# Attention, a routed and a dense feed-forward in one kernel: side work of the weights taken at full pace behind the routing, and one scale worked out inside it

## Chip, cores and metric

The kernel runs on one core of a Trainium2 chip. The metric is the device time of one execution in microseconds; of several runs the median counts. Time before: 695.2 us, median of three runs (694.49 to 697.42).

## What is computed

Three parts follow each other, for 3072 tokens of 384 values:

```python
# 1: linear attention, 4 batches, 8 heads, 768 steps, 48 values a head
cur   = einsum('bhd,bhe->bhde', u * kt, vt)
y[t]  = einsum('bhd,bhde->bhe', rt, state + cur)
state = w * state + einsum('bhd,bhe->bhde', kt, vt)
# 2: routing: all (token, expert) logits in falling order; a token goes to the first
#    of 8 experts that still has room (384 tokens each)
logits = x @ w_gate
h = maximum(x[mask] @ w1[e], 0); out[mask] = h @ w2[e]      # F = 1024
# 3: dense, with w1, w2, w3 of 384 x 768 and w_out of 768 x 384
h = maximum(maximum(x @ w1, x @ w2), x @ w3); out = h @ w_out
```

All of it is float32. The products of parts 2 and 3 run in float16 with each operand as a high and a low half, so one product is three matmuls for each 128 rows of the contraction: high by high, low by high, high by low. A matrix therefore needs **side work** before its first use: it is loaded in blocks of 768 KB, its largest magnitude is found, a power of two is made of that as its scale, and it is split into halves.

## The kernel before, in words

Attention comes first (to about 160 us), then the routing, which works on 24 x 8 logits a partition (to about 198 us), then the eight experts one after another, each with its share of part 3. TensorE (PE) does the products, ScalarE (ACT) the high halves, VectorE (DVE) the low halves, GpSimd (POOL) gathers and scatters of tokens, SyncE (SP) issues the loads.

**An expert** has four steps, in class Experts. `first` (8 products of nine matmuls, L925-932) gives the hidden layer, whose halves `ht` ACT and DVE write. `second` (3 products of 24, L934-962) gives `x`, whose scale DVE works out from the peaks `part` ("layer" scale). `third` (6 groups of 3 products of nine, L964-985) multiplies by the three matrices V. Of a group, ACT takes the first product out of its bank (`top`, L977), DVE the other two (L979); then ACT and POOL write the halves `gt`. Three banks `pg` hold these products, so each product waits until the one three before it is taken out. `fourth` (3 times 18 matmuls into `px`, L987-1013) multiplies by the output matrix WO. For the first expert `first` is written chunk by chunk of 128 tokens: five banks are filled from each chunk while `turn` (L863-897) writes the chunk's halves `xt`.

**Side work** is a list, made by the planner `Feed` (L497-578) when the program is written, and so is the order of every engine. `weight` (L643-704) gives the items of one expert's matrix: four squares on ACT that find the peak (`look`), three items of the scale (`scaled`: collect, share, done), then splits (`upper` on ACT, L684, `lower` on DVE, L688). `double` (L706-788) gives those of a V or of WO, which come as 64-bit numbers and are made float32 first: `magnitude` on ACT, `shift` (L739), `low` (L746) and `sign` (L755) on DVE, then squares, scale, splits (L780, L783). `Feed.take` (L562) runs items between the products against a budget of time: `side` (L1026) works out a pace from how much is left and when it is due (by tags: 0.2 the second expert's second matrix, 1 the last V, 1.5 WO, 2 and on the later experts), and what a step spends over its budget is carried as a debt to the next. `flush` runs all that is left of a tag. Four buffers `stage` hold the blocks; `Feed.ahead` (L538) writes a block's load into SP's queue when its first use is at most 6 items off and its buffer's last use is written.

In the routing, three `round`s and `settle` run on DVE and PE in turn. Between their steps stand `idle` steps of a generator, `inputs` (L812-828), which works out the scale of the tokens, and of the first four squares of the second expert's second matrix, two in each of the first two rounds (`aside`, L1262). A branch (L1411) skips more rounds, which the data does not need.

```python
        def side(time, part=1.0):
            clock[0] += time
            pace = max((feed.rest(tag) / max(due(tag) - clock[0] - SLACK[0] - SLACK[1] * feed.waits(tag), time) for tag in tags
                        if tag <= limit[0] and feed.left(tag)), default=0.0)
            feed.take(limit[0], min(SLACK[2] * pace * time, part * room[time]), None, time, APART)
```

Of the kernel before, what the change touches and what calls it, by code (L numbers as in the profile page):

```python
# [496 lines left out]
class Feed:  # L497


    SLOTS, AHEAD, LAG = 4, 6, 1.4  # L500

    def __init__(self):
        self.items, self.blocks, self.cost, self.at, self.loaded, self.spare, self.plan = [], [], [], 0, 0, 0.0, []
        self.now, self.ready = 0.0, 0.0

# [22 lines left out]
    def close(self):  # L528
        for tag, f, pe, blocks, cost in self.plan:
            self.cost.append((self.cost[-1] if self.cost else 0.0) + cost)  # L530
            for b in blocks:
                if b.first is None:
                    b.first = len(self.items)
                    self.blocks.append(b)
                b.last = len(self.items)
            self.items.append((tag, f, pe))
        self.plan = []

    def ahead(self, most=99):
        while self.loaded < min(most, len(self.blocks)):  # L540
# [45 lines left out]
class Experts:  # L586
# [53 lines left out]
    def mark(self, st):  # L640
        st["sent"] = self.feed.now

    def weight(self, e, which):  # L643

        nc = self.nc
        st = {"sent": 0.0}
        if which == 0:
            src, kb, n, store = self.w1d, self.KD, F, self.W1
            blocks = [self.block(src, e * DM * F + j * 512, [[F, 128], [128 * F, kb], [1, 512]], False)
                      for j in range(2)]  # L650
        else:
            src, kb, n, store = self.w2d, self.KF, DM, self.W2
            blocks = [self.block(src, e * DM * F + j * 4 * 128 * DM, [[DM, 128], [128 * DM, 4], [1, DM]], False)
                      for j in range(2)]

        def look(j):
            def go():
                if j == 0:
                    st["peaks"] = self.wp.tile([128, 4], F32, name=f"wpeak{which}")
                self.square(blocks[j // 2].get()[:, j % 2 * 768:j % 2 * 768 + 768], st["peaks"][:, j:j + 1])  # L660
                if j == 3 and not self.early:
                    self.mark(st)
            return go

        def column(out):
            nc.vector.tensor_reduce(out, st["peaks"], AX.X, OP.max)

        def powers(top):
            yield from self.sc.powering(top, 3, True, st)
            st["w"] = self.wpool[e % 2].tile([128, 2, kb, n], F16, name=f"w{which}", bufs=1)  # L670
            store[e] = (st["w"], st["f"])

        def part(j, q):
            if which == 0:
                return blocks[j].get()[:, q * 512:q * 512 + 512], [st["w"][:, t, q, j * 512:j * 512 + 512] for t in range(2)]
            k = 4 * j + 2 * q
            return blocks[j].get()[:, q * 768:q * 768 + 768], [
                st["w"][:, t, k:k + 2].rearrange("p k n -> p (k n)") for t in range(2)]

        parts = [(j, q) for j in range(2) for q in range(3 - which)]  # L680

        def upper(n):
            raw, (hi, _) = part(*parts[n])
            nc.scalar.activation(hi, raw, AF.Copy, scale=st["s"])  # L684

        def lower(n):
            raw, (hi, lo) = part(*parts[n])
            nc.vector.scalar_tensor_tensor(lo, raw, st["s"], hi, op0=OP.mult, op1=OP.subtract)  # L688

        def split(n):  # L690
            def go():
                if n < len(parts):
                    upper(n)
                if n:
                    lower(n - 1)
            return go

        def uses(n):
            return [blocks[parts[i][0]] for i in (n - 1, n) if 0 <= i < len(parts)]

        looks = [(look(j), False, [blocks[j // 2]], 0.9) for j in range(4)]
        return (looks + self.scaled(st, column, powers, blocks)
                + [(split(n), st if n == 0 and not self.early else False, uses(n), 0.6 + 0.3 * which)
                   for n in range(len(parts) + 1)])

# [105 lines left out]

    def inputs(self):  # L812

        sc, K = self.sc, self.K
        nc, peak, out = self.nc, sc.tile(), {}
        nc.vector.tensor_reduce(peak, K.norms, AX.X, OP.max)
        yield
        p = sc.psum()
        nc.tensor.transpose(p[:1, :128], peak, K.identf)
        yield  # L820
        most = sc.tile(shape=(1, 1))
        nc.vector.tensor_reduce(most, p[:1, :128], AX.X, OP.max)
        p = sc.psum()
        nc.tensor.matmul(p[:, :1], K.onesf[:1, :], most, start=True, stop=True)
        yield
        yield
        yield from sc.powering(p[:, :1], 7, True, out)
        K.xs, K.xf = out["s"], out["f"]

    def plan(self, late):  # L830

        feed = self.feed = Feed()
        self.early = False
        parts = [(0.2, self.weight(1, 1), None)] + [(1, self.double(i), 0) for i in late]
        parts[-1] = (1, parts[-1][1] + [(self.common, False, [], 1.5)], None)
        parts.append((1.5, self.double(3), 0))
        for e in range(2, E):
            parts += [(e, self.weight(e, 0), 7), (e + 0.3, self.weight(e, 1), 6)]
        feed.chain(parts)
        feed.close()  # L840
        feed.ahead(Feed.SLOTS)

    def open(self, ctx):
        tc = self.tc
# [65 lines left out]
            return self.psum.tile([128, CAP], F32, name="pg", bufs=3)  # L910
        return self.psum.tile([128, CAP], F32, name="ps", bufs=2)

    def first(self, e, wide=False, ahead=0):

        nc = self.nc
        h = self.act.tile([128, 2, self.KF, CAP], F16, name="ht", bufs=1)
# [1 line left out]
        w = self.W1[e][0]  # L918
        ps = [self.bank(f, wide) for f in range(ahead)]
        if ahead:  # L920
            for a, _ in enumerate(self.turn(e, True)):
                for f in range(ahead):
                    self.product(ps[f], w, slice(f * 128, f * 128 + 128), self.XT[e], self.KD,
                                 slice(a * 128, a * 128 + 128))
        for f in range(self.KF):  # L925
            if f < ahead:
                p = ps[f]
# [83 lines left out]
    def run(self):  # L1011
# [14 lines left out]
        def side(time, part=1.0):  # L1026

            clock[0] += time
            pace = max((feed.rest(tag) / max(due(tag) - clock[0] - SLACK[0] - SLACK[1] * feed.waits(tag), time) for tag in tags
                        if tag <= limit[0] and feed.left(tag)), default=0.0)  # L1030
            feed.take(limit[0], min(SLACK[2] * pace * time, part * room[time]), None, time, APART)

# [7 lines left out]
                feed.run()  # L1040

        self.gather(1)
        first = self.first(0, True, 5)
        for _ in range(5):
            next(first)
            clock[0] += F1
# [54 lines left out]
class Routing:  # L1101
# [11 lines left out]
    def fill(self):  # L1113
# [12 lines left out]
        part = t("part", [128, 1], I32)  # L1126
        nc.gpsimd.iota(part, [[0, 1]], base=0, channel_multiplier=1)
        self.i128 = count("i128", [[1, 128]], [128, 128], F16)
        self.token = t("token", [128, NT], F16)
        nc.gpsimd.iota(self.token, [[C, NT]], base=-N // 2, channel_multiplier=1, allow_small_or_imprecise_dtypes=True)  # L1130
        self.i24 = count("i24", [[1, NT]], [128, NT], F16)
        i8 = count("i8", [[0, J], [1, E]], [128, J, E])
        i25 = count("i25", [[1, NT + 1]], [128, NT + 1])
# [133 lines left out]
    def settle(self):  # L1267
# [32 lines left out]
        with nc.allow_low_precision(reason="whole numbers of up to 12 bits"):  # L1300
# [9 lines left out]
        nc.vector.tensor_tensor(col, af[:, :, None].to_broadcast([128, NT, NT]),  # L1310
                                self.i24[:, None, :].to_broadcast([128, NT, NT]), OP.is_equal)
        bent = col.rearrange("p (m q) n -> p m q n", q=4)[:, :, 2]
        nc.gpsimd.tensor_tensor(bent, bent, self.token.rearrange("p (m q) -> p m q", q=4)[:, :, 2, None]
                                .to_broadcast([128, NT // 4, NT]), OP.mult)
        rows = []
        for m in range(NT):
# [181 lines left out]
```

## Time and profile before

| | before |
|---|---|
| median of three runs | 695.2 us |
| the profiled execution, its time | 698.42 us |
| its span, first to last instruction | 696.7 us |
| PE busy | 650.7 us, 93% |
| DVE busy | 401.3 us, 58% |
| ACT busy | 351.8 us, 50% |
| POOL busy | 241.9 us, 35% |
| mean granted TensorE clock | 0.95 |

Times of rows are microseconds from the span's start. PE is the matmuls, PEld the weight loads beside them. A row of a timeline gives start, length, engine, line, operation, output<-input and how many instructions were merged; in brackets stands how long the engine sat idle before it, and what ended that. A row with a count is the whole stretch of these instructions. A granted clock of 1.00 is 2.4 GHz, of 0.50 it is 1.2 GHz.

### The profile page before, as it was taken

The numbers are of one execution on the slowest core, as the hardware profiler recorded it, in microseconds if no ns is written. First come the engines' busy times: TensorE is split into PE (matmuls) and PEld (weight loads), VectorE is DVE, ScalarE is ACT, GpSimd is POOL, SyncE is SP. The second block draws the span as 40 slices with busy tenths as digits, with TensorE's granted clock in tenths as the row PEclk, the third lists the DMA queues.
The fourth block names the chain that finished last, engine by engine and source line by source line (L and its number), as shares of the span: only waits on it lengthen the run. The fifth ranks groups of instructions, "written<-read, shape, count | busy, mean of one in ns | idle before, by whom it ended". The sixth has DMA issues, their size and how long they took to land.

```text
span 696.7 us, 14406 instructions
## 1 busy us (share of the span) xinstructions
PE 650.7 (93%) x5667; PEld 432.2 (62%) x5667; DVE 401.3 (58%) x1055; ACT 351.8 (50%) x785; POOL 241.9 (35%) x271
## 2 busy tenths in 40 slices
PE   6999998998689998799999999999999999999996
PEld 4788787887476554356666656666665666666663
DVE  7687997785715957646466454635636553551321
ACT  3576566643415556367466547446464535342321
POOL 6999999970150003113023112202212111110222
PEclk9889999996569999799999999999999999999999
DMA  8876867503035516116134310620611220000000
GB/s 225 277 254 215 291 207 229 177 35 115 1 107 123 184 45 176 39 69 159 49 123 87 117 58 24 162 88 35 156 48 70 46 92 1 34 1 1 35 1 34
DMA packets 54763, 72.98 MB, mean 105 GB/s; under 512 B 21408, under 2 KB 42016, under 8 KB 54688
## 3 DMA queue, kind: packets, MB, share of 16 engines
q1 hardware_dynamic: 51616, 62.55, 29.0%
q0 software_dynamic: 3072, 9.44, 4.8%
q8 instruction: 46, 0.75, 0.4%
q14 instruction: 29, 0.24, 0.1%
HBM read 58.41 MB, written 9.44 MB: 97 GB/s over the span
## 4 chain that ended last, share of the span: by engine, by line
PE 54%; issue 7%; DVE 5%; ACT 4%; POOL 1%; POOLq 0%; DVEq 0%; ACTq 0%
PE pg L904 25%; PE ps L904 20%; PE px L997 8%; ACT w L684 1%; DVE top L979 1%; POOL gt L984 1%; ACT junk L617 1%; DVE da L746 1%; DVE x2s L960 0%; ACT gt L983 0%; DVE ht L932 0%; DVE v L783 0%; DVE sc L430 0%; DVE da L739 0%; POOL out_dram L1002 0%
## 5 line engine op out<-in xcount | busy, mean ns | idle before, releaser
L904 PE MATMUL pg<-x2s,v 128*128 128x384 f16 x1296 | 218.2, 326 | 5.3 <-ACT top L977 3.3
L904 PEld LDWEIGHTS <-v 128*128 128x128 f16 x1296 | 126.6, 98 | 90.9 <-issue 6.0
L984 POOL TENSOR_TENSOR gt<-top,gt 128x384 f16<-128x384 f32 x48 | 44.5, 927 | 349.2 <-ACT gt L983 295.6
L904 PEld LDWEIGHTS <-w 128*128 128x128 f16 x1242 | 117.4, 99 | 73.7 <-issue 2.3
L688 DVE SCALAR_TENSOR_TENSOR w<-stage,sc,w 128x512 f16<-128x512 f32 (+1 forms) x80 | 72.4, 930 | 59.2 <-ACT w L684 59.2
L979 DVE SCALAR_TENSOR_TENSOR top<-pg,sc,top 128x384 f32<-128x384 f32 x96 | 59.1, 615 | 74.3 <-PE pg L904 63.6
L904 PE MATMUL ps<-ht,w 128*128 128x384 f16 x576 | 94.9, 326 | 1.7 <-DVE ht L932 1.7
L904 PE MATMUL ps<-xt,w 128*128 128x384 f16 (+1 forms) x540 | 88.8, 318 | 0.2 <-ACT xt L895 0.2
L997 PE MATMUL px<-wo,gt 128*128 128x384 f16 x432 | 76.4, 337 | 5.9 <-ACT wo L780 2.3
L983 ACT ACTIVATE gt<-top 128x384 f16<-128x384 f32 x48 | 25.1, 522 | 109.5 <-DVE top L979 109.5
L997 PEld LDWEIGHTS <-gt 128*128 128x128 f16 x432 | 43.1, 101 | 38.0 <-issue 9.2
L684 ACT ACTIVATE w<-stage,sc 128x512 f16<-128x512 f32 (+1 forms) x80 | 61.4, 798 | 2.2 <-DVE sc L468 2.2
L617 ACT ACTIVATE junk<-stage 128x768 bf16<-128x768 f32 x64 | 53.6, 838 | 5.1 <-DMA stage<-in_moe_w_dram 4.1
L932 DVE SCALAR_TENSOR_TENSOR ht<-ps,ht 128x384 f16<-128x384 f32 x56 | 31.0, 555 | 32.2 <-ACT ht L931 32.1
L1002 POOL DMA_INDIRECT out_dram<-o,ids x24 | 23.9, 995 | 47.1 <-ACT o L1000 47.1
L977 ACT ACTIVATE top<-pg,sc 128x384 f32<-128x384 f32 x48 | 27.7, 577 | 20.7 <-PE pg L904 18.2
L230 DVE TENSOR_TENSOR am<-pA,mask 128x512 f32<-128x512 f32 x48 | 30.7, 680 | 8.6 <-PE pA L227 8.6
L943 ACT ACTIVATE x<-ps 128x384 f32<-128x384 f32 x24 | 11.8, 491 | 47.0 <-PE ps L904 47.0
L931 ACT ACTIVATE ht<-ps 128x384 f16<-128x384 f32 x56 | 26.8, 482 | 15.8 <-PE ps L904 15.4
L1000 ACT ACTIVATE o<-px,sc 128x384 f32<-128x384 f32 x24 | 13.9, 581 | 39.1 <-PE px L997 35.8
L129 POOL TENSOR_TENSOR rt<-rt,tr 128x512 f32<-128x512 f32 x22 | 33.5, 1524 | 0.0
L227 PE MATMUL pA<-rt,kt 64*128 64x128 f32 x384 | 30.1, 292 | 2.2 <-DVE am L230 1.9
(236 smaller groups left out, 876.6 us busy)
## 6 DMA issues: line engine op xcount, KB each, us to landing
stage<-in_moe_w_dram SPq DMA_DIRECT2D x41, 768.0 KB, 5.3
kn<-in_k_dram SPq DMA_DIRECT2D x24, 192.0 KB, 5.1
rn<-in_r_dram SPq DMA_DIRECT2D x24, 192.0 KB, 4.9
v<-in_v_dram SPq DMA_DIRECT2D x24, 192.0 KB, 3.3
rt<-in_rt_dram SPq DMA_DIRECT2D x48, 96.0 KB, 3.4
x_rows<-x SPq DMA_DIRECT2D x24, 192.0 KB, 2.7
stage<-in_moe_w_out_dram SPq DMA_DIRECT2D x3, 768.0 KB, 5.6
xg<-x_rows,ids POOLq DMA_INDIRECT x24, 4.2
```

The lines of the kernel that those rows point to most:

```text
L129: (engine or self.nc.gpsimd).tensor_mul(self.RT[i], self.RT[i], self.tr)
L227: nc.tensor.matmul(pa[s][:, j, :], kt[FULL[s], j * C:(j + 1) * C], rt[FULL[s], j * C:(j + 1) * C], start=True, stop=True, skip_group_check ...
L230: nc.vector.tensor_mul(am[:, s], pa[s], self.mask[:, None, :].to_broadcast([128, NP, C]))
L617: self.nc.scalar.activation(self.K.junk, x, AF.Square, accum_out=total)
L684: nc.scalar.activation(hi, raw, AF.Copy, scale=st["s"])
L688: nc.vector.scalar_tensor_tensor(lo, raw, st["s"], hi, op0=OP.mult, op1=OP.subtract)
L904: nc.tensor.matmul(p[:, rows], w[:, wi, k, cols], x[:, xi, k, rows], start=k == 0 and wi + xi == 0, stop=k == kb - 1 and xi == 1, skip_gro ...
L932: nc.vector.scalar_tensor_tensor(h[:, 1, f], p, 0.0, h[:, 0, f], op0=OP.max, op1=OP.subtract)
L977: nc.scalar.activation(t, p, AF.Copy, scale=self.ratio[i])
L979: nc.vector.scalar_tensor_tensor(t, p, self.ratio[i], top, op0=OP.mult, op1=OP.max)
L984: nc.gpsimd.tensor_sub(gt[:, 1, g], top, gt[:, 0, g])
L997: nc.tensor.matmul(p, gt[:, gi, g, a * 128:(a + 1) * 128], self.WO[:, wi, g, :], start=g == 0 and gi + wi == 0, stop=g == self.KG - 1 and ...
```

## The change

Five things, all in what is written where:

1. In the routing the generator `inputs` goes on after the tokens' scale with the same steps for the second expert's second matrix (`self.later`, a call of the new `across`), so that its scale is worked out in the third round by two small products on PE. The items collect, share and done leave the list.
2. Eight items of side work are written into the first expert's `first` by a new argument `between`: one split before the chunks, four more behind the second chunk (these are all five of the second expert's second matrix), three of the last V behind the third.
3. `side` takes pace 1 as long as anything up to WO (tag 1.5) is left.
4. This list's loads may be written 12 items ahead (the attention's list keeps 6), and the first four are written at once (`fill`, where `ahead` wrote those that are needed within 6 items).
5. `settle` multiplies by `tokf` in float32 on POOL, where it used a float16 copy `token`, which is no longer made.

```diff
-    SLOTS, AHEAD, LAG = 4, 6, 1.4
-    def __init__(self):
+    SLOTS, LAG = 4, 1.4
+    def __init__(self, ahead=6):
+        self.AHEAD = ahead
...
+    def fill(self):
+        while self.loaded < min(self.SLOTS, len(self.blocks)):
+            self.blocks[self.loaded].load()
+            self.loaded += 1
...
-    def weight(self, e, which):
+    def weight(self, e, which, routed=False):
...
-        return (looks + self.scaled(st, column, powers, blocks)
+        if routed:
+            self.later = lambda: self.across(column, powers)
+        return (looks + ([] if routed else self.scaled(st, column, powers, blocks))
...
     def inputs(self):
+        K, out = self.K, {}
+        yield from self.across(lambda t: self.nc.vector.tensor_reduce(t, K.norms, AX.X, OP.max),
+                               lambda top: self.sc.powering(top, 7, True, out))
+        K.xs, K.xf = out["s"], out["f"]
+        yield
+        yield from self.later()
+
+    def across(self, column, powers):
         sc, K = self.sc, self.K
-        nc, peak, out = self.nc, sc.tile(), {}
-        nc.vector.tensor_reduce(peak, K.norms, AX.X, OP.max)
+        nc, peak = self.nc, sc.tile()
+        column(peak)
         yield
...
-        yield from sc.powering(p[:, :1], 7, True, out)
-        K.xs, K.xf = out["s"], out["f"]
+        yield from powers(p[:, :1])
...
-        feed = self.feed = Feed()
+        feed = self.feed = Feed(12)
...
-        parts = [(0.2, self.weight(1, 1), None)] + [(1, self.double(i), 0) for i in late]
+        parts = [(0.2, self.weight(1, 1, True), None)] + [(1, self.double(i), 0) for i in late]
...
-        feed.ahead(Feed.SLOTS)
+        feed.fill()
...
-    def first(self, e, wide=False, ahead=0):
+    def first(self, e, wide=False, ahead=0, between=lambda a: None):
...
         if ahead:
+            between(-1)
             for a, _ in enumerate(self.turn(e, True)):
...
+                between(a)
...
-            pace = max((feed.rest(tag) / max(due(tag) - clock[0] - SLACK[0] - SLACK[1] * feed.waits(tag), time) for tag in tags
+            pace = 1.0 if feed.left(1.5) else max((feed.rest(tag) / max(due(tag) - clock[0] - SLACK[0] - SLACK[1] * feed.waits(tag), time) for tag in tags
...
-        first = self.first(0, True, 5)
+        first = self.first(0, True, 5, lambda a: self.aside({-1: 1, 1: 4, 2: 3}.get(a, 0)))
...
-        self.token = t("token", [128, NT], F16)
-        nc.gpsimd.iota(self.token, [[C, NT]], base=-N // 2, channel_multiplier=1, allow_small_or_imprecise_dtypes=True)
...
-        nc.gpsimd.tensor_tensor(bent, bent, self.token.rearrange("p (m q) -> p m q", q=4)[:, :, 2, None]
+        nc.gpsimd.tensor_tensor(bent, bent, self.tokf.rearrange("p (m q) -> p m q", q=4)[:, :, 2, None]
```

Lines of the changed kernel are up to 17 higher for the same code. The order of three places follows.

DVE at the end of the third round (`pick` is the last step of the round's search, `pen` the first that uses its result `pt`, which PE makes of `pick`). Before:

```order
L1250 SCALAR_TENSOR_TENSOR hit,pick<-rank,goal 96x8
L1256 SCALAR_TENSOR_TENSOR val,pick<-hit,top 96x8
L1258 SCALAR_TENSOR_TENSOR pick<-pick,least 96x1
L1264 TENSOR_TENSOR pen<-nl,pt 128x192
L1265 SCALAR_TENSOR_TENSOR nl<-pen,nl 128x192
L1271 TENSOR_REDUCE best<-nl 128x24
```

Changed:

```order
L1265 SCALAR_TENSOR_TENSOR hit,pick<-rank,goal 96x8
L1271 SCALAR_TENSOR_TENSOR val,pick<-hit,top 96x8
L1273 SCALAR_TENSOR_TENSOR pick<-pick,least 96x1
L838 TENSOR_REDUCE sc_3034<-px 1x1
L454 TENSOR_SCALAR sc_3038<-px 128x1
L1279 TENSOR_TENSOR pen<-nl,pt 128x192
L1280 SCALAR_TENSOR_TENSOR nl<-pen,nl 128x192
L1286 TENSOR_REDUCE best<-nl 128x24
```

Two steps of the scale now stand between `pick` and `pen`: the largest of 128 peaks, and the first step of the power, which reads a `px` that PE writes in between from the former.

DVE from the second expert's tokens (`xr`) to its first hidden values (`ht`); `w` is the second expert's second matrix, `da` and `wo` the last V on its way to float32, and the rows from L949 (L966) on the first expert's layer scale. Before, from the matrix's splits on (ahead of them stand `xr` and the steps of the matrix's scale):

```order
L688 SCALAR_TENSOR_TENSOR w_4494<-stage,sc_4487,w_4494 128x768 x4
L739 TENSOR_SCALAR da<-da 128x768
L746 SCALAR_TENSOR_TENSOR da<-stage,da 128x768
L755 SCALAR_TENSOR_TENSOR wo<-stage,da 128x768
L422 MEMSET sc_4569 128x32
L949 TENSOR_REDUCE sc_4569<-part 128x1
L430 STREAM_TRANSPOSE sc_2826<-sc_4569 32x32 x4
L431 TENSOR_REDUCE sc_4570<-sc_2826 32x1
L932 SCALAR_TENSOR_TENSOR ht<-ps,ht 128x384
```

Changed:

```order
L892 SCALAR_TENSOR_TENSOR xr<-xg_2819,sc_2926,xr 128x384
L763 SCALAR_TENSOR_TENSOR wo<-stage,da 128x768
L747 TENSOR_SCALAR da<-da 128x768
L754 SCALAR_TENSOR_TENSOR da<-stage,da 128x768
L763 SCALAR_TENSOR_TENSOR wo<-stage,da 128x768
L422 MEMSET sc_4572 128x32
L966 TENSOR_REDUCE sc_4572<-part 128x1
L430 STREAM_TRANSPOSE sc_2824<-sc_4572 32x32 x4
L431 TENSOR_REDUCE sc_4573<-sc_2824 32x1
L949 SCALAR_TENSOR_TENSOR ht<-ps,ht 128x384
```

The four splits and their scale have left this place (they stand in the first expert's `first`), and the last V is two `sign` steps along.

ACT from the second expert's last hidden values to its third step; `junk,peaks<-wo` are squares of the last V, `x` and `junk,part` the three products of `second`, `v` the last V's high halves, `top` the first product of the first expert's `third`, `da` the magnitudes of WO. Before:

```order
L931 ACTIVATE ht<-ps 128x384
L943 ACTIVATE x_4706<-ps 128x384
L944 ACTIVATE junk,part<-ps 128x384
L617 ACTIVATE junk,peaks_4563<-wo 128x768 x2
L943 ACTIVATE x_4706<-ps 128x384
L944 ACTIVATE junk,part<-ps 128x384
L943 ACTIVATE x_4706<-ps 128x384
L944 ACTIVATE junk,part<-ps 128x384
L780 ACTIVATE v_84<-wo,sc_4778 128x768 x3
L977 ACTIVATE top_4838<-pg,sc_4823 128x384
L724 ACTIVATE da<-stage 128x768
```

Changed:

```order
L623 ACTIVATE junk,peaks_4415<-wo 128x768
L948 ACTIVATE ht<-ps 128x384
L960 ACTIVATE x_4718<-ps 128x384
L961 ACTIVATE junk,part<-ps 128x384
L960 ACTIVATE x_4718<-ps 128x384
L961 ACTIVATE junk,part<-ps 128x384
L788 ACTIVATE v_84<-wo,sc_4752 128x768 x3
L960 ACTIVATE x_4718<-ps 128x384
L961 ACTIVATE junk,part<-ps 128x384
L994 ACTIVATE top_4837<-pg,sc_4822 128x384
L732 ACTIVATE da<-stage 128x768 x2
```

The last two squares have moved ahead of the last `ht`, the three `v` ahead of the third product, and a second magnitude of WO stands right behind the first.

## Rows read from the trace of the kernel before

**Rows 1.** Busy time by stretch: start:end, length, busy us (instructions) of each engine, clock, DMA.
```profile
core 0: us, PE busy (x) PEld busy (x) DVE busy (x) ACT busy (x) POOL busy (x), PEclk, DMA share, GB/s
198.00:237.40 39.40, 38.81 (x315) 27.33 (x316) 22.94 (x60) 19.07 (x38) 5.34 (x6) 0.93 0.54 152
...
256.90:282.70 25.80, 22.95 (x135) 13.14 (x135) 20.59 (x46) 16.04 (x32) 8.23 (x8) 1.00 0.49 138
...
289.50:300.20 10.70, 10.70 (x49) 5.63 (x49) 4.02 (x21) 1.17 (x3) 2.16 (x4) 0.73 0.10 38
...
308.70:690.00 381.30, 379.60 (x2331) 227.64 (x2330) 183.81 (x498) 184.36 (x373) 72.56 (x95) 1.00 0.22 64
```

**Rows 2.** PE's timeline, second step of the second expert to the first expert's fourth step.
```profile
239.03 11.86 PE L904 MATMUL ps<-ht,w 128*128 128x384 f16 x72 [1.66 <-DVE ht L932]
250.73 3.41 PE L904 MATMUL pg<-x2s,v 128*128 128x384 f16 x20
...
256.88 7.50 PE L904 MATMUL pg<-x2s,v 128*128 128x384 f16 x45 [0.38 <-ACT top L977]
...
286.08 2.08 PE L997 MATMUL px<-wo,gt 128*128 128x384 f16 x6 [0.63 <-DVE wo L783]
289.50 10.66 PE L997 MATMUL px<-wo,gt 128*128 128x384 f16 x47 [1.34 <-DVE wo L783]
```

**Rows 3.** Chain of work that ended last: start, length, what (27 matmuls at full clock).
```profile
346.88 4.39 PE pg L904 x27
```

**Rows 4.** Timelines of PE and DVE in the routing's first and third round.
```profile
168.93 0.59 PE L1260 MATMUL pt<-same,pick 96*128 96x8 f32 x2
169.45 0.58 PE L824 MATMUL px<-sc,onesf 1*128 1x1 f32 x2
...
182.23 0.59 PE L1260 MATMUL pt<-same,pick 96*128 96x8 f32 x2
...
182.86 0.35 DVE L1264 TENSOR_TENSOR pen<-nl,pt 128x192 f32<-128x192 f32 x1 [0.68 <-PE pt L1260]
```

**Rows 5.** Timelines of POOL, DVE and PE: end of the routing, first chunks.
```profile
188.22 0.43 POOL L1313 TENSOR_TENSOR col<-col,token 128x144 f16<-128x144 f16 x1 [32.64 <-ACT gap L1320]
...
200.05 1.14 DVE L896 SCALAR_TENSOR_TENSOR xt<-px,sc,xt 128x384 f16<-128x384 f32 x2 [6.68 <-ACT xt L895]
205.21 0.62 DVE L896 SCALAR_TENSOR_TENSOR xt<-px,sc,xt 128x384 f16<-128x384 f32 x1 [4.02 <-ACT xt L895]
...
206.91 0.67 PE L904 MATMUL ps<-xt,w 128*128 128x128 f16 x9
```

**Rows 6.** DVE's timeline, second expert's first step.
```profile
223.62 3.81 DVE L688 SCALAR_TENSOR_TENSOR w<-stage,sc,w 128x768 f16<-128x768 f32 x4 [4.26 <-ACT w L684]
...
238.42 0.55 DVE L932 SCALAR_TENSOR_TENSOR ht<-ps,ht 128x384 f16<-128x384 f32 x1
```

**Rows 7.** Timelines of DVE and ACT at the start of the first expert's third step.
```profile
252.74 2.88 DVE L783 SCALAR_TENSOR_TENSOR v<-wo,sc,v 128x768 f16<-128x768 f32 x3 [3.94 <-ACT v L780]
...
256.25 0.58 ACT L977 ACTIVATE top<-pg,sc 128x384 f32<-128x384 f32 x1 [1.89 <-DVE sc L804]
```

**Rows 8.** A group by line and shape, 250.7 to 289.5: busy us, mean ns, idle before.
```profile
L617 ACT ACTIVATE junk<-stage 128x768 bf16<-128x768 f32 x4 | 3.4, 840 | 0.1
```

**Rows 9.** DVE's timeline: token halves without and with POOL's gathers beside them.
```profile
215.03 1.68 DVE L877 SCALAR_TENSOR_TENSOR xr<-xg,sc,xr 128x384 f16<-128x384 f32 x3
...
265.79 1.93 DVE L877 SCALAR_TENSOR_TENSOR xr<-xg,sc,xr 128x384 f16<-128x384 f32 x3 [0.63 <-ACT xr L876]
```

**Rows 10.** POOL's timeline: one of the gathers beside the first chunks.
```profile
201.42 0.95 POOL L861 DMA_INDIRECT xg<-x_rows,ids  x1 [0.30 <-issue]
```

**Rows 11.** Loads issued at 160.5 and 161.0: count, KB each, us to landing; and ACT's first square.
```profile
stage<-in_moe_w_dram SPq DMA_DIRECT2D x1, 768.0 KB, 4.6
...
stage<-in_moe_w_dram SPq DMA_DIRECT2D x1, 768.0 KB, 6.2
...
167.72 0.84 ACT L617 ACTIVATE junk<-stage 128x768 bf16<-128x768 f32 x1
```

More of the change, by code (lines that the diff above doesn't have):

```diff
@@ L660, in go @@
                 self.square(blocks[j // 2].get()[:, j % 2 * 768:j % 2 * 768 + 768], st["peaks"][:, j:j + 1])
-                if j == 3 and not self.early:
+                if j == 3 and not (self.early or routed):
                     self.mark(st)
```

## The prediction

> **What bounds the kernel now.** I read the stretches first. From 308.7 us to 690, PE is busy 379.6 of 381.3 us at full clock [rows 1]: nothing that happens beside it can shorten that, and the order of all engines there is the same in both kernels. From 198 to 237.4 PE is busy 38.8 of 39.4 us. What is left lies between 237.4 and 308.7, where the side work of the last V and of WO has to be done before PE can go on. PE's timeline shows the waits one by one [rows 2]. The first (1.66 us, ended by DVE's `ht`) holds the second expert's second step at 239.03. The second group of the first expert's third step starts at 256.88, though the step began at 250.73 and three products take 4.39 us [rows 3], so 1.76 us were lost on the way. From there to 282.7 PE is busy 22.95 of 25.8 us. Then the fourth step waits for WO's halves: it has done 7 matmuls when the last wait ends at 289.50, and does the other 47 at a mean clock of 0.73 [rows 1, 2].
>
> So the question is how much earlier each of these four places is reached. The sums are made against the profiled execution (698.42 us, of which 696.7 is span); it stands 3.2 us above the median of 695.2, so I take the difference and put it on the median.
>
> **The routing: 0.9 us lost.** The new scale costs DVE some twelve tiny steps, nearly all of them in waits. One is not: in the third round `pen` now stands behind a step that reads a product which PE makes last. Before, `pen` starts at 182.86, 0.04 us after PE's 0.59 us that began at 182.23. The same extra product in the first round started 0.52 us behind the one before it and took 0.58 us [rows 4]. So it ends near 183.33, the step behind it takes some 0.2 us, and `pen` starts at 183.55: 0.7 us late, and with it everything up to the gather. Four more steps stand on DVE between the flag's load and the branch, some 0.75 us; DVE sat idle for 6.68 us before its first work behind the branch [rows 5], so they are hidden unless PE waits for DVE at the branch, which I allow 0.2 us. POOL's product with a float32 operand lies on the path to the token numbers; it took 0.43 us with float16 [rows 5], and I bound the rest by 0 and by its own length again, nearer 0 since it is short and its width hardly grows. Together 0.9, between 0.5 and 1.6. The float16 copy that POOL no longer makes at the start is hidden there by an idle POOL.
>
> **The five splits in the first expert's `first`: nothing.** They take 3.81 us of DVE [rows 6]. Between its second and third chunk DVE has 4.02 us idle [rows 5], and ACT more. The third chunk's halves would begin at most 0.1 us later, and PE begins with them only at 206.91, with the high half. Behind them the three items of the last V take DVE until the first `ht`, as idle before.
>
> Here a rule speaks against the change. Beside these splits POOL issues the gathers for the next experts, 0.95 us each, three of them in that gap [rows 10]. Where DVE's two-operand steps ran beside gathers, three took 1.93 us instead of 1.68 [rows 9], 15% more; at this rate four splits take 4.4 us and the third chunk is still in time. The Trainium skill, "SBUF — State Buffer", section "Who interferes with whom", says that a DVE instruction with two inputs from SBUF and a GpSimd instruction that reads SBUF exclude each other for their whole length. By it the three gathers would push the splits back by 2.85 us; that is my third rival.
>
> **Second expert, start of its second step: 1.66 us gained.** Before, DVE comes to the layer scale of the first expert only behind four splits, which end at 227.4, and three steps of V [rows 6]. These splits, 3.81 us, are gone from there, and two of V's steps are done while DVE idles in the first expert's second step. The scale then starts as soon as ACT has delivered the last peak, and the eight `ht` follow PE. Keeping the distances of the old trace between these steps, the sixth `ht` ends near 236.3 instead of 238.97 [rows 6], before PE needs its bank at 237.4. What is late next is ACT: two squares now stand ahead of the last `ht`, and the second waits for DVE's last `sign`. I find the last `ht` at 238.4, and PE needs it as its eighth matmul at 238.5. So the gain is 1.66, with 0.5 as its lower end.
>
> **Start of the third step: 1.76 us gained.** ACT now splits the last V ahead of the third product, while PE works. Before, this began only when PE was done; DVE's halves followed from 252.74 for 2.88 us, then the ratios, and the first `top` at 256.25 [rows 7]. In the new order ACT splits 2.85 us before the step begins, DVE ends 1.0 us after it begins, and the first `top` starts 1.6 us after it, when its product has just ended (1.46). The fourth product needs it only at 4.39, so the three waits go.
>
> **Third step and WO: 1.8 us gained.** The work is the same, moved by one item: a `shift` and the first DVE `top` come before the fourth product instead of behind it. Against that, three of the next matrix's four squares (0.84 us each) now stand ahead of ACT's halves of the fourth group, where two stood [rows 8]. I laid the new order out with the old durations, from the step's start: the second group's last `top` ends at 10.4, the third's at 16.9; the squares run from 19.8 to 22.7, so the fifth group's first `top` ends at 24.1; its DVE `top`s at 26.3 and 27.4; WO's scale is ready at 29.9; its halves are done on ACT by 32.7, on DVE two by 32.8 and the last, behind a `top` and an `x2s`, at 36.2. Counted from the fourth product that is 31.8, where before it was 32.6 (289.50 minus 256.88) [rows 2]: 0.8 us gained. PE has then done 13 matmuls instead of 7, and the other six save 6 times 0.163 (4.39 over 27): 1.0 us. The clock falls as before, since PE still waits in two pieces, and the stretch at half clock behind the hold stays.
>
> **The sum:** 1.66 + 1.76 + 1.8 - 0.9 = 4.3 us. The profiled execution would be 694.1, the median **690.9 us**, 0.6% less. The more distant loads cost nothing: SP issues more of them before it is needed for the second expert's tokens. Pace 1 alone does little, as the eight items written into `first` and the four squares are booked as a debt of some 10 us, so no item runs until the third product of the first expert's second step.
>
> **Rivals.** 0.5% (3.5 us) is about what a measurement of this kernel can tell from no change.
>
> *Given back in the third step.* There PE, DVE and ACT wait for each other in turn, and the third square moves ahead. If the hold ends no earlier and the squares stand in for the gain before, only 1.66 + 1.76 - 0.9 = 2.5 us stay, less if the squares ahead of the last `ht` cost some: 692.7. For it: PE idles only 2.85 of 25.8 us there. Against: the layout above.
>
> *The clock stays up.* If PE's shorter idle before WO's first half lets the clock stand, the 47 matmuls' 10.66 us [rows 2], of which 7.64 are their time at full clock, show the price: 3.0 us more, 687.9. For it: 12 matmuls run in a row between the waits. Against: before, it fell within an idle stretch hardly longer.
>
> *The port.* With the splits pushed back 2.85 us, the third chunk's low half ends near 208.5 and is needed at 207.2: 1.3 us of the gain go, 692.2. It would decide where each gather holds a split for its whole length; [rows 9] show 0.25 us for three such steps.
>
> *Slower: the first square waits for its block.* Four loads start at 160.5 instead of two. If all four share the engines, the first lands with the last; ACT's first square, at 167.72, stands ahead of the second round's steps on ACT, and the whole routing waits. Two loads landed at 165.1 and 167.2 [rows 11], 2.1 us apart, so four end near 171.4 at that pace: 3.7 us lost, 694.6. Past a landing at 172.0 it is slower than before, at 175 it is 698.2. Against it: the first did land two microseconds before the second, as if one followed the other.
>
> **How the numbers follow.** My forecast has 0.52, of which 0.40 lie beyond 0.5% and 0.12 within, since its terms may each miss by half a microsecond or more; given back 0.20, the clock 0.15, the port 0.07, the square 0.06 (0.04 of it beyond 0.5%). Faster is 0.40 + 0.15 = 0.55, slower 0.04, the same 0.41. The range takes in the clock's case and, above, the given-back case with the lower ends of the second expert's term and the routing: 687.5 to 695.0.
>
> **What would show it.** The wait of 1.66 us ahead of the second expert's second step is gone; the third step runs its first four products without a wait of 0.3 us or more; `pen` of the third round starts about 1.3 us after `pick`'s product began, against 0.63; DVE's four splits end before 207; the last hold of the fourth step is still ended by DVE's `wo`, about 32 us after the fourth product, with 13 matmuls done. It is wrong if the third step takes over 32 us from start to end, if a PE wait of over 1 us stands at the last `ht`, or if ACT's first square starts after 168.5.

## The result, and the profile after

The changed kernel takes **689.24 us** (median of four runs, 687.97 to 692.0); the kernel before, run beside it, takes 696.31. The ratio is 0.9906, with a 95% interval of 0.9883 to 0.993. A second comparison gave 689.72 against 696.25, 0.9915 (0.9894 to 0.9937). So it is faster by 6.5 to 7.1 us; I had forecast 4.3. The profiled execution took 689.38 us, its span 687.7.

PE's timeline, routing's end to the second expert's third step (it answers to [rows 2] and to the waits of [rows 5]):

```profile
197.38 1.51 PE L901 MATMUL px<-identf,xg 128*128 128x128 f32 x6 [1.41 <-DVEq L1426]
...
235.85 12.15 PE L919 MATMUL ps<-ht,w 128*128 128x384 f16 x72
247.84 13.33 PE L919 MATMUL pg<-x2s,v 128*128 128x384 f16 x81
261.63 9.12 PE L919 MATMUL pg<-x2s,v 128*128 128x384 f16 x54 [0.46 <-ACT top L994]
272.11 1.62 PE L919 MATMUL pg<-x2s,v 128*128 128x384 f16 x9 [1.37 <-ACT top L994]
274.32 3.09 PE L919 MATMUL pg<-x2s,v 128*128 128x384 f16 x18 [0.58 <-DVE top L996]
279.01 0.32 PE L1014 MATMUL px<-wo,gt 128*128 128x384 f16 x1 [1.60 <-ACT wo L788]
280.06 3.73 PE L1014 MATMUL px<-wo,gt 128*128 128x384 f16 x12 [0.73 <-DVE wo L791]
284.40 6.82 PE L1014 MATMUL px<-wo,gt 128*128 128x384 f16 x41 [0.61 <-DVE wo L791]
...
299.77 4.55 PE L919 MATMUL pg<-x2s,v 128*128 128x384 f16 x27 [1.23 <-ACT top L994]
```

The 1.66 us ahead of the second expert's second step are gone, and the third step runs its first nine products (81 matmuls) without a wait. New is a wait of 1.37 us ahead of its last three products. The last wait of the fourth step ends at 284.40 with 13 matmuls done, as forecast; but the other 41 then run at 0.166 us each, where 47 took 10.66 us before [rows 2].

Busy time by stretch (columns as in [rows 1]); the last row answers to the last of [rows 1]:

```profile
197.40:235.85 38.45, 38.29 (x315) 26.94 (x316) 25.63 (x54) 21.32 (x43) 7.06 (x6) 0.95 0.46 132
247.84:277.24 29.40, 26.96 (x163) 15.82 (x162) 21.93 (x54) 17.72 (x36) 8.63 (x8) 1.00 0.56 121
...
284.40:291.06 6.66, 6.66 (x41) 4.00 (x41) 3.11 (x20) 1.16 (x2) 2.16 (x4) 1.00 0.15 53
299.77:687.70 387.93, 379.60 (x2331) 227.65 (x2330) 183.71 (x498) 184.77 (x373) 73.52 (x96) 1.00 0.23 64
```

Behind 299.77 nothing differs: PE is busy 379.60 us in both, and from the start of that row to the end of the span it is 387.93 us here and 388.0 before (696.7 less 308.70). The gain lies ahead of it. I read the same stretches, between the starts of the same rows of PE, in every profile:

| profile | routing | to 2nd expert's second step | that step | third and fourth step | from first token product |
|---|---|---|---|---|---|
| before | 35.80 | 40.63 | 11.70 | 49.27 | 101.60 |
| **changed** | 35.97 | 38.47 | 11.99 | 43.22 | 93.68 |
| changed, again | 36.45 | 38.76 | 11.99 | 43.21 | 93.96 |
| scale alone | 36.19 | 39.09 | 13.11 | 47.80 | 100.00 |
| no items in `first` | 36.43 | 38.47 | 13.10 | 44.88 | 96.45 |
| changed, old loads | 36.37 | 37.29 | 11.99 | 46.58 | 95.86 |
| before, new loads | 35.50 | 39.10 | 11.70 | 49.01 | 99.81 |
| changed, old pace | 36.35 | 38.80 | 11.70 | 48.48 | 98.98 |
| before, pace 1 | 35.62 | 40.64 | 11.70 | 49.27 | 101.61 |

The routing starts anywhere between 159.87 and 164.81 us over the profiles, whatever the kernel. So 1.2 us of the 9.0 between the two spans is no work of the change. In the column behind it, "changed, old loads" and "before, new loads" had full clock (2.4 GHz, granted 1.00) over the first 5 us of the chunks, where before and changed had 0.52 and 0.59; that takes 1.2 and 1.5 us off.

### The profile page after: what moved, and what is told of

It reads as the page before. It is cut to its first block, busy times and chain, and to the rows that moved or that the text cites. A ratio compares the mean times of both kernels' runs of the same rounds, so it can differ in the third digit from the quotient of the medians.

```text
span 687.7 us, 14407 instructions
## 1 busy us (share of the span) xinstructions
PE 646.8 (94%) x5670; PEld 430.1 (63%) x5670; DVE 398.8 (58%) x1048; ACT 352.2 (51%) x785; POOL 243.6 (35%) x270
## 4 chain that ended last, share of the span: by engine, by line
PE 54%; issue 8%; DVE 4%; ACT 3%; POOL 1%; POOLq 0%; DVEq 0%; ACTq 0%
PE pg L919 25%; PE ps L919 21%; PE px L1014 8%; ACT junk L623 1%; DVE top L996 1%; POOL gt L1001 1%; DVE x2s L977 1%; ACT w L690 1%; ACT gt L1000 0%; DVE ht L949 0%; DVE wo L791 0%; POOL out_dram L1019 0%; DVE gt L763 0%; DVE sc L430 0%; DVE da L747 0%
## 5 line engine op out<-in xcount | busy, mean ns | idle before, releaser
L1014 PE MATMUL px<-wo,gt 128*128 128x384 f16 x432 | 74.1, 331 | 4.5 <-ACT wo L788 1.6
L949 DVE SCALAR_TENSOR_TENSOR ht<-ps,ht 128x384 f16<-128x384 f32 x56 | 31.0, 555 | 32.3 <-ACT ht L948 32.3
L227 PE MATMUL pA<-rt,kt 64*128 64x128 f32 x384 | 31.9, 304 | 0.6 <-POOL rk L193 0.2
```

The costliest lines, as they stand in the source:

```text
L227: nc.tensor.matmul(pa[s][:, j, :], kt[FULL[s], j * C:(j + 1) * C], rt[FULL[s], j * C:(j + 1) * C], start=True, stop=True, skip_group_check ...
L949: nc.vector.scalar_tensor_tensor(h[:, 1, f], p, 0.0, h[:, 0, f], op0=OP.max, op1=OP.subtract)
L1014: nc.tensor.matmul(p, gt[:, gi, g, a * 128:(a + 1) * 128], self.WO[:, wi, g, :], start=g == 0 and gi + wi == 0, stop=g == self.KG - 1 and ...
```

## Experiments: the change taken apart

My theory was that the scale's three items, gone from the list, make the gain, since every later row of ACT and DVE then falls into its new place by itself. **Scale alone** (against the changed kernel; the float32 operand stays too):

```diff
-        feed = self.feed = Feed(12)
+        feed = self.feed = Feed()
...
-        feed.fill()
+        feed.ahead(Feed.SLOTS)
...
-            pace = 1.0 if feed.left(1.5) else max((feed.rest(tag) / max(...
+            pace = max((feed.rest(tag) / max(...
...
-        first = self.first(0, True, 5, lambda a: self.aside({-1: 1, 1: 4, 2: 3}.get(a, 0)))
+        first = self.first(0, True, 5, lambda a: None)
```

> The changed kernel with only the scale in the routing and the float32 operand left of the change: nothing is written into the first expert's first step, the pace is the old one, the loads are written as before. On ACT and DVE the five splits and three items of the last V then stand behind the first and second product of the first expert's second step; from there on every row stands as in the changed kernel. Theory (what gains is that the scale's three items, with the two waits that they bring, are gone from the list; where the eight items are written costs nothing, since DVE has 6.6 us idle ahead of the layer scale and they are 5.3 us): no wait of PE at the second expert's second step, 27 or more products of the third step ahead of its first wait, 689.2 us plus or minus 1. Rival (the early place of the eight items is what gains): the wait of 1.66 us at the second expert's second step stays, 691 to 693 us.

It took 696.58 us, ratio 1.0007 (0.9989 to 1.0025): nothing gained. The theory fell, and the rival's 691 to 693 us were missed too. (In the table it stands 1.6 us below before: its profiled execution, 694.9 us, is one of its faster ones.) ACT's timeline shows why, and PE's what it did:

```profile
223.36 0.94 ACT L732 ACTIVATE da<-stage 128x768 f32<-128x768 f32 x1 [1.92 <-DMA stage<-in_moe_w_dram]
...
273.59 0.84 ACT L623 ACTIVATE junk<-stage 128x768 bf16<-128x768 f32 x1 [2.96 <-DMA stage<-in_moe_w_dram]
```

```profile
238.23 10.72 PE L919 MATMUL ps<-ht,w 128*128 128x384 f16 x65 [1.25 <-ACT ht L948]
...
275.96 5.88 PE L919 MATMUL pg<-x2s,v 128*128 128x384 f16 x27 [4.29 <-ACT top L994]
```

The order is the new one, but the blocks are not there. In SP's queue two blocks of the last V stand behind the second expert's transposes, which wait for its tokens:

```profile
213.41 4.87 SPq L893 DMA_TRANSPOSE xt<-xr  x3
218.32 1.33 SPq L615 DMA_DIRECT2D stage<-in_moe_w_dram  x2
...
236.57 0.37 SPq L615 DMA_DIRECT2D stage<-in_moe_w_dram  x1
261.84 4.02 SPq L893 DMA_TRANSPOSE xt<-xr  x3
```

In the changed kernel five loads stand ahead of them, and two, not one, ahead of the next three transposes. ACT's second and longer wait (2.96 us, for a block of the third expert's first matrix) comes from that second place:

```profile
159.34 43.06 SPq L615 DMA_DIRECT2D stage<-in_moe_w_dram  x5
214.43 4.65 SPq L893 DMA_TRANSPOSE xt<-xr  x3
...
235.61 20.65 SPq L615 DMA_DIRECT2D stage<-in_moe_w_dram  x2
260.91 4.01 SPq L893 DMA_TRANSPOSE xt<-xr  x3
```

**No items in `first`** is this kernel with the new loads and pace 1; ACT's, DVE's and PE's rows are in the same order as with the scale alone.

> The changed kernel without the eight items in the first expert's first step; scale, pace 1, loads as changed. Its rows on ACT, DVE and PE stand in the same order as those of the run with the scale alone, but the loads are written early: two blocks of the last V ahead of the branch (there one), two of the third expert's first matrix ahead of the first expert's token transposes (there one). Theory (with the scale gone from the list, what limits is the loads): no wait for a DMA on ACT, no wait of PE at the second expert's second step, 689 to 690 us. Rival (the items must stand early): 0.7 us or more of wait at that step and 2 us or more of the gain lost, 691 us or more.

691.89 us, 0.9947 (0.9927 to 0.9968). No engine waits for a block any more, and by the table 3.6 us came back: the loads, since the order of the rows is the same. The other 2.8 us did not, and the rival holds: 1.1 us of them lie in the second expert's second step (13.10 us against 11.99), and 1.7 in the clock of the fourth step, of which more below. DVE can begin the items only when ACT has the first peak, and is through with them at 228.08; the layer scale starts at 228.27, 2.3 us behind its last peak, and PE waits 0.29 and 1.25 us:

```profile
236.93 1.30 PE L919 MATMUL ps<-ht,w 128*128 128x384 f16 x7 [0.29 <-DVE ht L949]
239.47 10.72 PE L919 MATMUL ps<-ht,w 128*128 128x384 f16 x65 [1.25 <-ACT ht L948]
```

My 6.6 us of idle DVE were not all to be had, as 3.02 us of them lie ahead of the first split.

**The loads by themselves**, undone in the changed kernel and done in the one before (the first two pairs of lines of the diff above, either way):

> The changed kernel with the loads written as before (at most 6 items ahead, no filling at the start); every other engine's rows as changed. The second block of the third expert's first matrix then stands behind three transposes on SP, as in the run with the scale alone. Theory: ACT waits some 3 us for it in the third step, PE some 4 us behind that, and the fourth step ends 4.6 us later, as there (47.8 us from the third step's start against 43.2): 693 to 695 us. Rival (the distance of the loads is worth nothing, as I had predicted): 689.2 us.

> The kernel before with the changed loads alone; every other engine's rows as before. Theory: no engine waits for a block there before, so nothing is gained, 695 to 696.5 us. Rival (earlier loads are a gain of their own): 693 us or less.

The first took 691.97 us, 0.9968 (0.9948 to 0.9989): in its third step ACT waits 1.72 us for the third expert's block and PE 3.04 us behind it, and the two steps take 3.4 us more (I had expected 4.6); half of that lies in the clock behind the waits, as in the next section (8.50 us for the 41 products). The second took 695.72 us, 1.0011 (0.9996 to 1.0027). Early loads gain nothing in the old order, and the new order loses 2.3 to 3.4 us without them.

**The pace** by itself, undone and done (third pair of lines):

> The changed kernel with the old pace. The eight items written into the first step book a debt of some 10 us, and with the old pace the last V is split behind the third product of the second expert's second step again, as before the change. Theory: the first group of the third step waits again, 1.5 to 2.5 us of the gain are lost, about 691 us. Rival (pace 1 does nothing): 689.2 us.

> The kernel before with pace 1 alone. Theory: the matrix's scale stays in the list and its three items wait for their peaks, so the four splits still stand ahead of the layer scale and the last V is split behind the third product: 1 us of gain at most, 695 to 697 us. Rival (full pace is what gains): at least 3 us faster than before, 693 us or less.

693.54 us, 0.9967 (0.9949 to 0.9986), and 694.59 us, 0.9981 (0.9963 to 0.9999). With the old pace the last V's halves are late again, and the two steps take 48.48 us; some 4 us of the gain are lost, more than I had expected. Alone the pace changes no stretch of the table by more than 0.01 us behind the routing. By its code it repays the debt that the items in `first` leave behind and has nothing to repay without them. The two runs without items agree with that: one has the old pace, one pace 1, and their ACT and DVE rows are in the same order.

## Experiments: the clock behind WO's halves

In the profile before, PE's clock is low from the middle of the fourth step's waits far into its products (two stretches, columns as in [rows 1]):

```profile
275.00:285.00 10.00, 6.96 (x42) 3.98 (x41) 5.54 (x20) 7.28 (x16) 1.82 (x2) 1.00 0.51 185
285.00:295.30 10.30, 8.31 (x26) 3.65 (x26) 7.42 (x25) 3.24 (x5) 2.04 (x4) 0.51 0.01 2
```

In the changed kernel half clock (1.2 GHz) lasts from 280.0 to 283.4, all of it between the first of these waits and the last, which ends at 284.40:

```profile
280.00:283.40 3.40, 3.34 (x11) 1.57 (x11) 2.30 (x5) 1.64 (x3) 0.94 (x2) 0.50 0.00 0
```

To price this, products of ones into an unread bank fill the waits, in the kernel before (20, 4 and 20 of them, as shown) and in the changed one (13, 5 and 20):

```diff
+            idle = self.psum.tile([128, CAP], F32, name="ps", bufs=2) if e + a == 0 else None
+            done = 0
             for g in range(self.KG):
                 for gi, wi in ((0, 0), (0, 1), (1, 0)):
+                    if idle is not None:
+                        warm(nc, K, idle, {0: 20, 1: 4, 7: 20}.get(done, 0))
+                    done += 1
```

> The kernel before with 44 products of ones into a bank that nobody reads, in the three waits of the first expert's fourth step (20, 4 and 20). They keep PE busy there and nothing else. Theory: the granted clock stays at 1.00, the 47 products behind the last wait take 7.6 to 7.8 us instead of 10.7, and the kernel gains 3 us: 692.5 us. Rival (the products behind the wait are held by something else than the clock, or the added products delay them): 695.5 us or more.

> The changed kernel with 38 products of ones into a bank that nobody reads, in the three waits of the first expert's fourth step (13, 5 and 20). Theory (the clock's fall is all that is left to win there, and it costs between nothing and 1.7 us): granted clock 1.00 there, 41 products in 6.8 us in every run, the median 0 to 1.7 us below that of the unchanged kernel of this call. Rival (products of ones collide with the waits): the last wait ends later and the median is higher.

> The changed kernel once more, as it is, to see how far the profiled execution can be taken for the usual one. In its first profile the half-clock stretch of 3.4 us lay inside the fourth step's waits and the 41 products behind the last wait took 6.82 us; in the run without the eight items the waits were the same and the stretch lay behind them, 8.50 us. Theory (where that stretch falls is chance): median 689 to 690.5 us, runs spread over 1.5 us or more. Rival (it is tied to this program): 689.2 us again, and 6.8 us for the 41 products.

Before, with them:

```profile
284.37 2.35 PE L385 MATMUL ps<-onesf 128*128 128x256 bf16 x20
286.82 7.80 PE L1002 MATMUL px<-wo,gt 128*128 128x384 f16 x47
```

The 47 take 7.80 us instead of 10.66, and the two steps 2.9 us less (46.39 against 49.27); the medians give 693.41 us, 0.9974 (0.9959 to 0.999), so 0.7 to 2.9 us. In the changed kernel the same cure does nothing: 0.9916 (0.9898 to 0.9934) with it, 0.9915 without, measured together. Its profile has full clock there, and the two steps take 43.22 us as without it:

```profile
280.96 2.11 PE L1019 MATMUL px<-wo,gt 128*128 128x384 f16 x12 [0.19 <-DVE wo L791]
285.31 6.82 PE L1019 MATMUL px<-wo,gt 128*128 128x384 f16 x41
```

So there the low stretch costs nothing, the lower end of that text's theory. Its rival fell: the last wait ends 36.56 us after the third step's start in both. The second profile of the changed kernel again has 6.82 us for the 41, and so has the first version of the next section, which is the same in this place. That is the rival of the last text, as far as three profiles go; the times do not part it from the theory, whose median and spread came out too (689.72 us, 688.63 to 692.1). In the run without items the low stretch lies behind the waits, although the last of them ends as far from the third step's start (36.54 us):

```profile
280.00:286.90 6.90, 2.77 (x16) 1.46 (x16) 5.32 (x11) 3.62 (x5) 0.94 (x2) 1.00 0.00 0
286.90:290.40 3.50, 3.50 (x13) 1.65 (x12) 2.83 (x18) 0.58 (x1) 1.10 (x2) 0.51 0.02 5
```

There the 41 take 8.50 us, 1.7 more. Why it falls inside in one kernel and behind in the other stays open; I have no run that moves it alone.

## Experiments: two further versions

In the **routing** the new scale's first power step stood ahead of `pen`. Moved behind it, into DVE's waits of `settle`:

```diff
-        self.idle(1 if src is self.K.raw else 3)
+        self.idle(1 if src is self.K.raw else (3, 3, 2)[n])
         self.aside((2, 2, 0)[n])
...
+        self.idle(2)
         held = self.small("heldc", [128, 2])
...
+        self.idle(3)
         at = self.small("at", [128, NT, E])
```

> The changed kernel with the first step of the second scale's power moved from ahead of the third round's penalty to behind it (its five tiny steps stand in two waits of the settling, two ahead of the count's copy, three ahead of the positions). Theory: the penalty starts 0.6 us earlier, and PE no longer waits for DVE at the branch, 0.15 us: 688.4 us. Rival (the five steps delay the positions by as much, some 0.18 us each, or PE's wait at the branch is set by another engine): 689.2 us or up to 0.4 more.

688.17 us, 0.9899 (0.9871 to 0.9928), against 0.9906 and 0.9915: the interval can't tell half a microsecond, the rows can. DVE's timeline of the changed kernel, and of this one:

```profile
180.34 0.27 DVE L838 TENSOR_REDUCE sc<-px 1x1 f32<-1x128 f32 x1
181.63 0.16 DVE L454 TENSOR_SCALAR sc<-px 128x1 int32<-128x1 int32 x1 [1.01 <-PE px L840]
181.70 0.35 DVE L1279 TENSOR_TENSOR pen<-nl,pt 128x192 f32<-128x192 f32 x1
```

```profile
180.04 0.35 DVE L1279 TENSOR_TENSOR pen<-nl,pt 128x192 f32<-128x192 f32 x1 [0.49 <-PE pt L1275]
...
181.49 0.15 DVE L454 TENSOR_SCALAR sc<-px 128x1 int32<-128x1 int32 x1
```

`pick`'s product began at 180.48 in the first and 179.41 in the second, so `pen` comes 1.22 and 0.63 us behind it; the routing takes 35.78 us instead of 36.0 to 36.45.

The wait of 1.37 us that the change left in the **third step** is due to three squares of the third expert's matrix, on ACT ahead of the fourth group's halves, from 267.80 to 270.68:

```profile
267.80 0.84 ACT L623 ACTIVATE junk<-stage 128x768 bf16<-128x768 f32 x1
...
269.74 0.84 ACT L623 ACTIVATE junk<-stage 128x768 bf16<-128x768 f32 x1
...
270.58 0.51 ACT L1000 ACTIVATE gt<-top 128x384 f16<-128x384 f32 x1
```

With the squares behind WO's splits in the list:

```diff
-        parts.append((1.5, self.double(3), 0))
+        parts.append((1.5, self.double(3), None))
```

> The changed kernel with the four squares of the third expert's first matrix behind WO's splits in the list, where they stood ahead of WO's scale. In the third step three squares (2.9 us with their sums) then no longer stand ahead of ACT's halves of the fourth group, and WO's scale follows its own peaks at once. Theory (from 267.8 us on the changed kernel's third step is held by ACT's squares, and the fourth by WO's halves behind them): no wait of PE of over 0.5 us from the third step's start on, and a fourth step without a wait, so from the third step's start to the fourth's end 36 to 38 us instead of 43.2; some of it may come back at the second expert's third step, whose splits now follow later: 683 to 686 us. Rival (the squares are only moved to where ACT is as short, ahead of the second expert's third step): the wait there grows from 1.23 us to 4 us or more, 688 us or more.

687.25 us, 0.9872 (0.9853 to 0.9892). The two steps take 40.54 us instead of 43.22, the wait ahead of the next third step stays at 1.22 (4 or more by the rival), and half of what I had expected has turned into new waits:

```profile
273.72 1.62 PE L919 MATMUL pg<-x2s,v 128*128 128x384 f16 x9 [0.63 <-DVE top L996]
275.69 1.62 PE L919 MATMUL pg<-x2s,v 128*128 128x384 f16 x9 [0.34 <-DVE top L996]
277.15 2.89 PE L1014 MATMUL px<-wo,gt 128*128 128x384 f16 x15
281.35 0.50 PE L1014 MATMUL px<-wo,gt 128*128 128x384 f16 x2 [1.31 <-ACT gt L1000]
```

```profile
277.52 1.94 DVE L791 SCALAR_TENSOR_TENSOR wo<-gt,sc,wo 128x768 f16<-128x768 f32 x2
279.38 1.36 DVE L996 SCALAR_TENSOR_TENSOR top<-pg,sc,top 128x384 f32<-128x384 f32 x2
```

WO is ready now, and the last group's `gt` is late: DVE does two halves of WO, 1.94 us, ahead of the last two `top`. Both versions at once:

> Both later versions at once: the second scale's power moved behind the third round's penalty, and the four squares behind WO's splits. Theory (the two save at different places, 0.5 us in the routing and 2.7 us in the third and fourth steps): routing 35.8 us from its first product to the first token product, 40.5 us from the third step's start to the fourth's end, about 0.5 us below the version with the squares alone, 0.5% below the changed kernel: a ratio of 0.986 to the kernel before. Rival (one of them gives back what the other gains): 0.988 or more.

685.66 us, 0.9859 (0.9825 to 0.9893), as the theory has it; routing 35.65 us, the two steps 40.52. It is the lowest median, though its interval does not part it from the version with the squares alone.

## Why the forecast was right in sign and too small

- **Routing, 0.9 lost.** The eight profiles with the new scale in its first place average 36.29 us, the four without it 35.64: 0.65 lost. `pen` was 0.59 later (forecast 0.7). POOL's product with float32 takes 0.44 us where it took 0.43 [rows 5], so that bound's lower end was right. These means hide a part of the cost, since the first two rounds happened to be 0.2 us shorter in the eight. From the third round's `pick` product to the first token product the eight take 16.83 to 17.06 us and the four 15.97 to 16.17, on average 0.87 more: 0.59 for `pen`, the rest at the branch, where PE waits 1.31 to 1.58 us instead of 1.06 to 1.26. In the four PE's own sequencer (`PEq`) ends that wait, in seven of the eight DVE's (`DVEq`), for which I had allowed 0.2 us. The row before the change:

```profile
198.40 1.51 PE L886 MATMUL px<-identf,xg 128*128 128x128 f32 x6 [1.26 <-PEq L1411]
```

- **Splits in `first`, nothing.** They take 3.79 us from 200.09, done by 203.88, and the third chunk's halves follow at once. The rival of the port fell.
- **Second expert, 1.66 gained.** To its second step 2.16 us are gone, in that step 0.29 come back, 1.87 in all. Of the 2.16, 0.34 lie in the first chunks (10.68 us against 11.02), where the clock differed.
- **Third step's start, 1.76 gained.** Right: no wait up to the ninth product. The step as a whole went from 31.79 to 29.40 us (its 18 products take 26.3), although the squares ahead of the fourth group brought 1.37 of wait; the rival "given back in the third step" fell.
- **Third step and WO, 1.8 gained: here it failed.** The last hold ended 32.2 us after the fourth product (forecast 31.8), with 13 matmuls done, so that part gave 1.4. The step that failed is "the clock falls as before ... and the stretch at half clock behind the hold stays". It fell, for 3.4 us instead of some 10, inside the waits, and the products behind the hold ran at full clock. That is 2.9 us, the price of the rival on the clock, which I had given 0.15, with a different course: I had it not fall at all. It is nearly the whole of what the forecast lacks; the other terms missed by up to 0.4 us, in both directions.
- **"The more distant loads cost nothing."** True, and beside the point: my layout of the new order took the blocks for loaded, and only the new loads make them so. Without them 2.3 to 3.4 us go.
- **"Pace 1 alone does little."** True alone; with the items in `first` 4 us hang on it.

By the table, 101.60 less 93.68 gives 7.9, less 0.65 in the routing 7.3, beside 7.1 and 6.5 from the medians. The rival of the first square fell too: four loads stood where two had, and the square began at 165.83 with no wait for its block.

## What to carry to other kernels

The parts of a change in an order of work may be worth nothing one by one: here the scale, the loads and the pace alone came out between 0.1% slower and 0.2% faster, and with the items in `first` (not tried alone) they gave 0.9%; whoever tries them singly throws all of them away. When work is moved ahead, read the queue of its loads as well, and what stands ahead of them there. And when products follow a wait, count them at the clock that their rows show: here the last wait ended 2.2 us earlier in the two steps, and the products behind it took 2.9 us less by the clock, for a reason that no run shows.

## What the hardware did that I had not expected

Beside the four splits, POOL's gathers paid, not DVE:

```profile
199.94 0.94 POOL L876 DMA_INDIRECT xg<-x_rows,ids  x1 [0.30 <-issue]
201.19 1.66 POOL L876 DMA_INDIRECT xg<-x_rows,ids  x1 [0.30 <-issue]
203.15 1.55 POOL L876 DMA_INDIRECT xg<-x_rows,ids  x1 [0.30 <-issue]
```

The two that began during a split took 1.66 and 1.55 us instead of 0.95 [rows 10], and the splits 3.79 instead of 3.81 [rows 6]. The gather of 199.94 began ahead of the first split (200.09); it took its 0.94, and the split did not wait for its end. In all eight profiles with the items in `first`, two gathers of this place take 1.34 to 1.66 us; in the six without them none behind the first takes more than 0.95.

The Trainium skill, "SBUF — State Buffer", section "Who interferes with whom", also says that the order of issue decides which of the two engines blocks. With that the two later gathers agree, the one at 199.94 does not. And the 0.71 and 0.60 us are less than one split's length (0.95), for which by that section the other engine should be shut out.
